# Second batch's keys in load buffers of their own, all key and value loads issued earlier, six bias groups ahead of the steps

## The chip, the cores and the metric

The kernel runs on one core of a Trainium2 chip. The metric is the device time of one launch in microseconds. The engines of the core that matter here are TensorE (PE, with its weight loads as PEld), VectorE (DVE), ScalarE (ACT), GpSimd (POOL) and SyncE (SP); nearly all transfers are issued on SP's queue, and 16 DMA engines carry them out. An engine takes its instructions strictly in the order in which they are written: this kernel is scheduled by hand, and nothing reorders it.

## The reference, cut to what matters

Three layers follow each other: attention with a learned position bias, a token and channel mixer, and a routed expert layer. The change touches the attention alone.

```python
# q, k, v: (2, 8, 576, 64): B batches, H heads, S positions, D
scores = scale * np.matmul(q, k.transpose(0, 1, 3, 2))
x = (psi_rel / psi_i)[..., None]              # of the two positions
bias = np.maximum(x @ w1 + b1, 0.0) @ w2      # (576, 576, 8 heads), 32 hidden units
scores = scores + bias.transpose(2, 0, 1)[None, :, :, :]
attn = softmax(scores)                        # row maximum, exp, row sum
out = np.matmul(attn, v)
# then the mixer (_moe_ref) and the routed experts (_moe2_ref)
```

## The kernel before, in words

**Steps.** The 576 query rows are cut into four tiles of 128 rows and a tail of 64. The tail comes first: `its` is tail, 0, 1, 2, 3. For each of the five there are eight steps, one for each pair of heads (four pairs of batch 0, then four of batch 1), so steps 0 to 7 are the tail and step 8 is the first of tile 0. A step s does the scores and softmax of its own pair, the transposes of the probabilities of step s-1, and the product with the values of step s-2 (its output transpose too). In the tail phase step s also transposes and splits the keys of pair s+2 (`key_T`, `key_split`), since those are needed for the first time then.

**Bias.** The bias of a row tile is the same for both batches. It is made in groups of 16 query rows, 36 in all: groups 0 to 3 for the tail, 4 to 11 for tile 0, and so on. `bias_hidden` makes the hidden layer of a group in four parts (`hidden0` to `hidden3`), each on DVE, ACT or POOL as `ENGINE` says. `bias_mm` multiplies it on PE (L500), ACT copies the result to an `ev` tile (L503, two `ev` buffers), and one DMA on SP (L511; two half-size ones at L509 for the tail) spreads it over the partitions of the bias tile. The softmax of a step (`softmax_tile`: DVE L337 adds the bias and takes the row extreme, ACT L340 the exponential) reads the whole bias tile of its row tile. So step 0 needs groups 0 to 3 landed, and step 8 needs groups 4 to 11.

**What sets the order.** `ORDER["start"]` is the list of work ahead of step 0, written out by hand; it holds the loads and `bias0` to `bias4`. Then each step runs a list of its phase. `AHEAD = 1` makes `ahead` = 5: five groups are done at the start and each later step does one (`gi`), so that group 11 is done in step 6 and step 7 does none. SP's queue is in order too: a DMA whose data isn't ready holds all that are written behind it. Each SP DMA also waits until the one eight places ahead of it has landed.

**Loads.** `load_k(i)` loads the keys of two pairs (five DMAs, 576 KB) into a ring of two buffers `kn`; `load_k(4)`, the first of batch 1, therefore waits for the transposes of the first keys, and `load_k(6)` for those of the second. `load_v(b)` loads the values of one batch (ten DMAs, 1152 KB). `load_q` loads queries; in step 4 the load for step 10 waits for a buffer that POOL's `tail_split` of step 5 frees. `query_rest` copies the split queries of a pair of steps into place with four DMAs (`qt<-qs`, L328).

Of the kernel before, what the change touches and what calls it, by code (L numbers as in the profile page):

```python
# [9 lines left out]
F32 = mybir.dt.float32  # L10
# [11 lines left out]
B, H, S, D = 2, 8, 576, 64  # L22
# [26 lines left out]
MROWS = E * CAP + 10 * 128  # L49

WARM = 3
AHEAD = 1
QRB = 2
TB = 2
QO = 3, 3, 3, 6

ORDER = {
    "start": "hidden0 const load_k2 tail_split0 hidden1 bias0 hidden2 bias1 key_T00 hidden3 zero key_T01 key_T11 key_T10 key_split0 tail_split1 bias2 hidden4 bias3 load_k4 hidden5 key_split1 tail_T bias4 load_v load_q".split(),
    "first": "scores0 hidden2 last_T prob_T0 values key_T0 normalize query_T tail_T query_split hidden1 hidden0 key_T1 bias_mm key_split out_T tail_split hidden3 query_rest".split(),
    "mixed": "hidden2 scores0 values tail_T query_T normalize hidden0 last_T prob_T0 key_T0 key_T1 query_split tail_split hidden1 key_split query_rest bias_mm out_T hidden3".split(),  # L60
    "bias": "query_T query_split hidden3 scores0 scores1 last_T values hidden0 query_rest hidden2 late bias_mm out_T mix prob_T0 prob_T1 hidden1 normalize".split(),
# [37 lines left out]
def body(ctx, tc, q, k, v, w1, b1, w2, wt1, wt2, wc1, wc2, wg, wl, mw1, mw2,  # L99
# [17 lines left out]
    with tc.manual_schedule():  # L117
        tok = ctx.enter_context(ExitStack())
        mix = TokenMix(nc, x)
        attention(tc, nc, tok, mix, q, k, v, w1, b1, w2, c_L, c_id, ident, x, wt1, wt2, prefill)  # L120
        if "x" in dbg:
            nc.sync.dma_start(dbg["x"], x)
        R = Routing(tc, nc, wg, wl, ident, c_tok, c_small, x2d, meta)
        X = Experts(tc, nc, R, Rings(tc, ctx, "big", side="right"), x_p, mw1, mw2, ident, x2d, meta, out)
        mixer(tc, nc, tok, mix, wc1, wc2, ident, x, R, X)
        if "x2" in dbg:
            nc.sync.dma_start(dbg["x2"], x2d)
        X.rest()
        X.close()
        R.close()  # L130


def attention(tc, nc, tok, mix, q, k, v, w1, b1, w2, c_L, c_id, ident, x, wt1, wt2, prefill):
# [9 lines left out]
    tw_p = pool(tok, "tokw")  # L143
    with ExitStack() as ctx:
        cst = pool(ctx, "acst")
        bias_p = pool(ctx, "bias", 2)
        nat_p = pool(ctx, "nat")
# [58 lines left out]


        nat = {}

        def load_k(i):  # L210

            b, pr = divmod(i, NP)
            n = nat_p.tile([128, 20, D], F32, name="kn", tag="kn", bufs=2)
            main, hs = n[:, 0:16].rearrange("p (n h) d -> p n h d", h=4), k[b, 2 * pr:2 * pr + 4]
            for j in range(NIT):
                nc.sync.dma_start(main[:, j], hs[:, 128 * j:128 * j + 128].rearrange("h p d -> p h d"))
            nc.sync.dma_start(n[0:64, 16:20], hs[:, 512:S].rearrange("h p d -> p h d"))
            for j in range(2):
                nat["k", i + j] = main[:, :, 2 * j:2 * j + 2], n[0:64, 16 + 2 * j:18 + 2 * j]

        def load_v(b):
            n = kv_p.tile([128, NIT + 1, H, D], F32, name=f"v{b}")


            nv, src = n.rearrange("p n (a e) d -> e p n a d", e=2), v[b].rearrange("(a e) p d -> e p a d", e=2)
            for e in range(2):
                r, z = (slice(64 * o, 64 * o + 64) for o in (e, 1 - e))
                nc.gpsimd.memset(nv[e][z, NIT], 0.0)
                for j in range(NIT):
                    nc.sync.dma_start(nv[e][:, j], src[e][64 * e + 128 * j:64 * e + 128 * j + 128])  # L230
                nc.sync.dma_start(nv[e][r, NIT], src[e][0:64] if e else src[e][512:S])
            nat["v", b] = n

        def load_q(it, i):

            b, pr = divmod(i, NP)
            n = nat_p.tile([128, 4, D], F32, name="qn", tag="qn", bufs=2)
            if it == NIT:
                tv = q[b, :, 512:S].rearrange("(a e) p d -> e p a d", e=2)
                for e in range(2):  # L240
                    nc.sync.dma_start(n[64 * e:64 * e + 64], tv[e])
                for j in range(NP):
                    nat["q", it, i + j] = n[:, j]
            else:
                nc.sync.dma_start(n, q[b, 2 * pr:2 * pr + 4, 128 * it:128 * it + 128].rearrange("h p d -> p h d"))
                nat["q", it, i] = n
# [271 lines left out]
        def fetch(p):  # L518
            n = p[1]
            if p[0] == 0:  # L520
                src = wt1[128 * n:min(128 * n + 128, S)]
            else:
                src = wt2[128 * n:128 * n + 128, HALF * p[2]:HALF * p[2] + HALF]
            raws[p] = fetch_f64(nc, nat_p, src, "kn", 2, p[0] == 0 and n == 4)
# [61 lines left out]
        first = NG - 8 * NIT  # L586
        ahead = first + AHEAD
        N = len(steps)
# [19 lines left out]
        def late_fetch(s):  # L608

            if pieces and any(f is decode for f, *_ in late.get(s, ())):  # L610
                fetch(pieces.pop(0))

        load_const()
        bias_setup()
        start = {
            "const": (bias_const,), "zero": (query_zero,), "load_k2": (load_k, 2), "load_k4": (load_k, 4), "load_v": (load_v, 0),
            "load_q": (load_q, *steps[NP]), "tail_T": (tail_T, *steps[0]),
        }
        for n in range(2):
# [11 lines left out]
        for s in range(N + 2):  # L631

            bias = gi < len(groups) and s < N and s >= B * NP * (its.index(groups[gi] // 8) - 1)
            at = lambda d, n=N: steps[s + d] if 0 <= s + d < n else None
            two = lambda d: (s + d) % 2 == 0 and s + d >= B * NP and at(d)
            hide = groups[gi + 1] if bias and gi + 1 < len(groups) else None
            todo = {
                "late": (late_step, (s,)), "mix": (mixes[s][0], mixes[s][1:]) if s in mixes else (None, None),
                "tail_split": (tail_split, at(2, B * NP)), "tail_T": (tail_T, at(1, B * NP)),
                "query_T": (query_T, two(QO[0])), "query_split": (query_split, two(QO[1])), "query_rest": (query_rest, two(QO[2])),  # L640
                "key_split": (key_split, at(2, B * NP)),
                "normalize": (normalize, at(0)), "last_T": (last_T, at(-1)),
                "values": (values, at(-2)), "out_T": (out_T, at(-2)),
                "bias_mm": (bias_mm, (groups[gi],) if bias else None),
            }
            for j in range(4):
                todo[f"hidden{j}"] = bias_hidden, hide is not None and (hide, (j,))
                todo[f"key_T{j}"] = key_T, j < 2 and at(2, B * NP) and (*at(2), j)
                todo[f"scores{j}"] = scores, at(0) and (*at(0), j)
                todo[f"prob_T{j}"] = prob_T, at(-1) and (*at(-1), j)  # L650
            if two(QO[3]):
                load_q(*steps[s + QO[3]])
            for name in ORDER["edge" if bias and s % (B * NP) == B * NP - 1 else "first" if s < 3 else "mixed" if s < B * NP else "bias" if bias else "plain"]:
                f, a = todo[name]
                if a:
                    f(*(a[1:] if f in (key_split, key_T) else a))
            gi += bias
            late_fetch(s - 1)
            if s == 1:
                load_k(6)  # L660
            if s == 2:
                load_v(1)
            if s == 10:
                prefill()
            if s == 8:
                for _ in range(2):
                    fetch(pieces.pop(0))
# [635 lines left out]
class Experts:  # L1303
# [6 lines left out]

    AHEAD = [[f"big{4 * a + c}.0" for c in range(4)] for a in range(2)]
    HIGH = [f"big{8 + c}.0" for c in range(4)], ["raw.0", "raw.1", "raw.2", "uT0a.0"]
    LOW = ["uT1a.0", *AHEAD[0][0:3]], [AHEAD[0][3], *AHEAD[1][0:3]]

# [11 lines left out]
    def guess(self):  # L1326
        nc = self.nc
        self.raw = [[self.place(n, F32) for n in names] for names in self.AHEAD]
        self.e = e = nc.values_load(self.R.picked[0:1, 0:1], engines=[SP], min_val=0, max_val=E - 1)
# [14 lines left out]
    def open(self):  # L1344
# [7 lines left out]
            (0, 0): cycle([*map(spot, self.HIGH[0]), own(0)]), (0, 1): cycle([*map(spot, self.LOW[0]), own(1)]),  # L1352
            (1, 0): cycle([*map(spot, self.HIGH[1]), spot(self.AHEAD[1][3])]), (1, 1): cycle([*map(spot, self.LOW[1]), own(2)]),
        }
# [408 lines left out]
```

## Time and profile before

| | |
|---|---|
| median of 3 runs | 583.69 us (582.85 to 583.7) |
| the profiled execution | 584.03 us; its span 582.3 us |
| busy share of the span: PE, DVE, ACT, POOL | 94%, 66%, 57%, 42% |
| chain that ended last, PE / DVE / DMA / issue / ACT | 65% / 12% / 7% / 5% / 5% |
| of it, bias transfers `bias<-ev` | 6% |

The busy shares are means over phases with different limits. The tail phase with its start takes the first 72 us; the four row tiles follow to about 220 us, then mixer and experts. The profile's page cuts the span into 40 slices of 14.6 us; in the first five DVE reads 5, 7, 8, 9, 5 tenths, and the page's DMA line 6, 9, 9, 7, 9. The time outside the span (584.03 less 582.3, 1.7 us) is launch and end.

### The profile page before, as it was taken

How to read it: one execution, taken by the hardware profiler on the slowest of the kernel's cores; microseconds unless marked ns; L12 is line 12 of the kernel's file. 1: busy time of each engine (PE TensorE's matmuls, PEld its weight loads, DVE VectorE, ACT ScalarE, POOL GpSimd, SP SyncE). 2: the span in 40 equal slices, each digit the busy share in tenths (PEclk: the TensorE clock that was granted, in tenths of full speed). 3: DMA queues.
4: the chain of work that ended last, by engine and by line, in shares of the span. 5: the costliest groups of instructions: out<-in, count | busy, mean ns of one | idle time of the engine just before them, and what ended most of it. 6: DMA issues, size and time to landing. Idle time of an engine off the chain costs nothing.

```text
span 582.3 us, 11959 instructions
## 1 busy us (share of the span) xinstructions
PE 545.5 (94%) x4306; PEld 430.3 (74%) x4306; DVE 383.9 (66%) x896; ACT 329.5 (57%) x608; POOL 242.1 (42%) x230
## 2 busy tenths in 40 slices
PE   7689699999899999989999999999999999999992
PEld 3366477777677887869999877787778778787871
DVE  5789588889887675698888535714473235668650
ACT  4678589789898793344444223221423257777760
POOL 4666547476555360044444300310014234657541
PEclk8979889999999999999999999999999999999997
DMA  6997988698697351143443020081002985566950
GB/s 162 130 173 126 142 158 165 132 177 157 127 147 126 77 154 38 37 138 120 148 161 126 1 91 0 1 302 61 19 18 43 370 299 175 147 230 245 367 185 12
DMA packets 72110, 79.90 MB, mean 137 GB/s; under 512 B 36822, under 2 KB 51420, under 8 KB 72044
## 3 DMA queue, kind: packets, MB, share of 16 engines
q1 hardware_dynamic: 67276, 73.72, 50.7%
q0 software_dynamic: 2176, 5.26, 2.7%
q8 instruction: 36, 0.59, 0.5%
q10 hardware_dynamic: 2592, 0.09, 0.3%
q14 instruction: 30, 0.25, 0.2%
HBM read 72.08 MB, written 5.34 MB: 133 GB/s over the span
## 4 chain that ended last, share of the span: by engine, by line
PE 65%; DVE 12%; DMA 7%; issue 5%; ACT 5%; SPq 2%; POOL 2%; ACTq 0%; POOLq 0%; DVEq 0%
PE ph L748 20%; PE po L748 16%; DMA bias<-ev 6%; PE py L748 5%; PE ps L500 5%; PE tp L425 4%; PE ps L359 3%; PE tp L410 3%; DVE t L337 2%; ACT t L340 2%; PE tp L748 1%; DVE K L272 1%; DMA mt<-meta 1%; PE tp L1448 1%; DVE raw L732 1%
## 5 line engine op out<-in xcount | busy, mean ns | idle before, releaser
L490 POOL TENSOR_SCALAR hd<-tabs,sc,negb 128x576 f32<-128x576 f32 x32 | 76.4, 2389 | 4.7 <-PE ps L500 3.0
L340 ACT ACTIVATE t<-t,st 128x576 f32<-128x576 f32 x72 | 55.4, 770 | 28.8 <-DVE st L337 28.4
L748 PE MATMUL po<-cw,h 128*128 128x512 f32 x272 | 67.3, 395 | 0.0
L337 DVE CUSTOM_DVE_ANT_0 t<-ps,bias 128x576 f32<-128x576 f32 x72 | 52.3, 751 | 16.1 <-DMA bias<-ev 6.6
L359 PE MATMUL ps<-K,qt 128*128 128x288 f32 x320 | 54.0, 309 | 4.4 <-DVE qt L199 3.5
L748 PEld LDWEIGHTS po<-cw,h 128*128 128x128 f32 x272 | 49.8, 188 | 10.0 <-issue 0.4
L1411 DVE TENSOR_TENSOR big<-raw,big 128x1024 fp32r<-128x1024 f32 x30 | 42.3, 1433 | 22.4 <-ACT big L1410 22.4
L500 PE MATMUL ps<-hd,wblk 128*32 128x288 f32 x576 | 47.7, 440 | 7.5 <-DVE st L337 6.5
L359 PEld LDWEIGHTS ps<-K,qt 128*128 128x128 f32 x320 | 45.0, 192 | 6.7 <-DVE qt L199 2.3
L425 PE MATMUL tp<-pt,v 128*64 128x128 f32 (+1 forms) x800 | 49.2, 268 | 0.6 <-DVE K L272 0.6
L748 PE MATMUL py<-big,hT 128*128 128x512 f32 x184 | 47.8, 400 | 0.4 <-POOL big L1411 0.4
L1189 POOL DMA_INDIRECT meta<-tokid,posi x10 | 10.0, 996 | 90.7 <-DVE tokid L1186 54.7
L425 PEld LDWEIGHTS tp<-pt,v 128*64 128x64 f32 x800 | 40.1, 137 | 8.1 <-issue 5.1
L1410 ACT CAST big<-raw 128x1024 fp32r<-128x1024 f32 x44 | 44.2, 1055 | 2.8 <-DMA big<-in_moe_w_dram 1.0
L748 PE MATMUL ph<-big,xT 128*128 128x512 f32 x168 | 42.9, 403 | 0.0
L490 DVE TENSOR_SCALAR hd<-tabs,sc,negb 128x576 f32<-128x576 f32 x69 | 42.2, 640 | 1.0 <-PE ps L500 0.9
L748 PEld LDWEIGHTS py<-big,hT 128*128 128x128 f32 x184 | 33.8, 188 | 8.6 <-POOL big L1411 0.9
L740 POOL TENSOR_TENSOR big<-wf,big 128x512 fp32r<-128x512 f32 x12 | 18.8, 1564 | 50.3 <-ACT big L739 50.3
L487 ACT ACTIVATE hd<-tabs,b1c,sc 128x576 f32<-128x576 f32 x43 | 36.9, 866 | 3.8 <-DVE sc L458 3.7
L1411 POOL TENSOR_TENSOR big<-raw,big 128x1024 fp32r<-128x1024 f32 x10 | 27.5, 2747 | 24.9 <-ACT big L1410 24.3
L748 PEld LDWEIGHTS ph<-big,xT 128*128 128x128 f32 x168 | 30.6, 189 | 8.6 <-issue 1.6
L500 PEld LDWEIGHTS ps<-hd,wblk 128*32 128x32 f32 x576 | 17.2, 115 | 24.1 <-DVE st L337 7.9
(302 smaller groups left out, 1204.7 us busy)
## 6 DMA issues: line engine op xcount, KB each, us to landing
raw<-in_moe_w_dram SPq DMA_DIRECT2D x48, 512.0 KB
raw<-in_moe_w_ch_dram SPq DMA_DIRECT2D x24, 512.0 KB
bias<-ev SPq DMA_DIRECT2D x32, 288.0 KB
qt<-qs SPq DMA_DIRECT2D x64, 128.0 KB
lw<-in_moe_w_dram SPq DMA_DIRECT2D x16, 512.0 KB
big<-in_moe_w_dram SPq DMA_DIRECT2D x8, 512.0 KB
lw<-in_moe_w_dram SPq DMA_DIRECT2D x16, 256.0 KB
big<-in_moe_w_dram SPq DMA_DIRECT2D x16, 256.0 KB
```

The source lines that it names most:

```text
L337: nc.vector.tensor_tensor_reduce(t.rearrange("p (a j) -> p a j", a=2), ps[:, :, 0:HALF], bs.rearrange("p (a j) -> p a j", a=2), op0=ALU.ad ...
L340: nc.scalar.activation(t, t, AF.Exp, bias=st[:, j:j + 1], scale=-1.0, accum_out=st[:, 2 + j:3 + j])
L359: nc.tensor.matmul(ps[:, hf, 0:HALF], lhsT=qt[:, j], rhs=K[k][:, hf * HALF:(hf + 1) * HALF], start=j == pairs[0][0], stop=j == pairs[-1][0])
L410: nc.tensor.transpose(tp[:, 128 * j:128 * j + 128], tt[:, o:o + 128], ident)
L425: nc.tensor.matmul(po[64 * h:64 * h + 64, 0:rhs.shape[1]], lhsT=lhsT, rhs=rhs, start=j == 0, stop=j == 4)
L487: nc.scalar.activation(hd[:, qq], Lt[:, o:o + S], AF.Relu, bias=b1c, scale=sc[:, c])
L490: eng.tensor_scalar(hd[:, qq], Lt[:, o:o + S], sc[:, c], negb, ALU.mult, ALU.max)
L500: nc.tensor.matmul(ps[32 * qq:32 * qq + 32, hf, 0:HALF], lhsT=wblk, rhs=hd[:, qq, hf * HALF:(hf + 1) * HALF], start=True, stop=True)
L740: nc.gpsimd.tensor_tensor(lo, src, hi.bitcast(F32), ALU.subtract)
L748: nc.tensor.matmul(out, lhsT=lhs[a], rhs=rhs[b], start=first and i == 0, stop=last and i == 2)
L1410: nc.scalar.copy(hi, raw)
L1411: (nc.gpsimd if c == 3 and t else nc.vector).tensor_tensor(lo, raw, hi.bitcast(F32), ALU.subtract)
```

## The change

The ring `kn` now holds only the keys of batch 0; those of batch 1 go into a new tile `later` of `tokw`, in the place (tag `w2s`) that the mixer's second token weights take from step 9 on. `load_k4` moves ahead of group 2's transfer, `load_v` ahead of group 3's, `load_k6` from the end of step 1 ahead of group 4's, and `load_v(1)` from step 2 to step 0. `AHEAD` becomes 2: group 5 and the hidden layer of group 6 are done at the start, and every tail step does the group that the next step did; step 6 does none. Group 5 counts as one of the start's for the choice of engines (`hidden_by`).

```diff
-AHEAD = 1
+AHEAD = 2
...
-    "start": "hidden0 const load_k2 tail_split0 hidden1 bias0 hidden2 bias1 key_T00 hidden3 zero key_T01 key_T11 key_T10 key_split0 tail_split1 bias2 hidden4 bias3 load_k4 hidden5 key_split1 tail_T bias4 load_v load_q".split(),
+    "start": "hidden0 const load_k2 tail_split0 hidden1 bias0 hidden2 bias1 load_k4 key_T00 hidden3 zero key_T01 key_T11 key_T10 key_split0 tail_split1 bias2 load_v hidden4 bias3 load_k6 hidden5 key_split1 tail_T bias4 load_q hidden6 bias5".split(),
...
         nat = {}
+        later = tw_p.tile([128, 2, 20, D], F32, name="kn2", tag="w2s")
...
-            n = nat_p.tile([128, 20, D], F32, name="kn", tag="kn", bufs=2)
+            n = later[:, i // 2 - 2] if b else nat_p.tile([128, 20, D], F32, name="kn", tag="kn", bufs=2)
...
-            if s == 1:
-                load_k(6)
-            if s == 2:
+            if s == 0:
                 load_v(1)
```

In the rows below `kn` are keys, `v` values, `qn` queries, `bias<-ev` a bias group's transfer. On SP's queue, around the tail's bias groups, this stood before (L509 the eight halves of groups 0 to 3, L511 group 4):

```order
L217 DMA kn<-in_k_dram 64x4x64
L509 DMA bias_185<-ev 16x4x576 x8
L216 DMA kn<-in_k_dram 128x4x64 x4
L217 DMA kn<-in_k_dram 64x4x64
L511 DMA bias_310<-ev 16x8x576
L230 DMA v_323<-in_v_dram 128x4x64 x4
L231 DMA v_323<-in_v_dram 64x4x64
```

and this stands now (all lines below the first insertion are one higher, and L510 is the tail's groups):

```order
L218 DMA kn<-in_k_dram 64x4x64
L510 DMA bias_186<-ev 16x4x576 x4
L217 DMA kn_104<-in_k_dram 128x4x64 x4
L218 DMA kn_104<-in_k_dram 64x4x64
L510 DMA bias_186<-ev 16x4x576 x2
L231 DMA v_278<-in_v_dram 128x4x64 x4
L232 DMA v_278<-in_v_dram 64x4x64
L231 DMA v_278<-in_v_dram 128x4x64 x4
L232 DMA v_278<-in_v_dram 64x4x64
L510 DMA bias_186<-ev 16x4x576 x2
```

The tail's eight transfers are cut in three: the third group stands behind the third load of keys, the fourth behind the ten loads of values too.

On SP's queue, around the last bias groups of tile 0 (steps 4 to 7; L245 loads queries, L328 puts the split queries in place), before:

```order
L245 DMA qn<-in_q_dram 128x4x64
L511 DMA bias_310<-ev 16x8x576
L328 DMA qt_104<-qs 64x2x256 x4
L511 DMA bias_310<-ev 16x8x576
L245 DMA qn<-in_q_dram 128x4x64
L511 DMA bias_310<-ev 16x8x576
L328 DMA qt_105<-qs 64x2x256 x4
```

and now:

```order
L246 DMA qn<-in_q_dram 128x4x64
L512 DMA bias_328<-ev 16x8x576
L329 DMA qt_105<-qs 64x2x256 x4
L512 DMA bias_328<-ev 16x8x576
L246 DMA qn<-in_q_dram 128x4x64
L329 DMA qt_106<-qs 64x2x256 x4
```

Behind the waiting load of queries there were three groups (9, 10, 11), and there are two (10, 11); the last now stands ahead of the next load of queries.

## Rows read from the trace of the kernel before

**Rows 1.** Busy time by stretch: PE, PEld, DVE, ACT, POOL, granted clock, DMA share, GB/s
```profile
16.00:18.00 2.00, 1.25 (x8) 0.34 (x6) 1.94 (x5) 1.14 (x2) 1.42 (x1) 1.00 0.15 25
28.00:36.00 8.00, 6.94 (x45) 4.57 (x45) 6.82 (x19) 6.17 (x11) 5.98 (x10) 0.57 1.01 170
36.00:44.00 8.00, 6.91 (x98) 5.21 (x97) 7.51 (x23) 5.69 (x12) 5.30 (x9) 1.00 1.21 169
66.00:72.00 6.00, 2.02 (x29) 1.61 (x29) 1.07 (x4) 0.98 (x2) 4.31 (x4) 0.77 1.14 140
```

**Rows 2.** Timeline of DVE around step 0: start, length, what, [idle before <- releaser]
```profile
21.19 0.29 DVE L199 TENSOR_SCALAR qt<-tp 128x128 fp32r<-128x128 f32 x1
24.44 0.76 DVE L337 CUSTOM_DVE_ANT_0 t<-ps,bias 128x576 f32<-128x576 f32 x1 [2.96 <-PE tp L262]
...
30.07 0.76 DVE L337 CUSTOM_DVE_ANT_0 t<-ps,bias 128x576 f32<-128x576 f32 x1
```

**Rows 3.** Timeline of PE: the scores of step 0
```profile
21.63 1.34 PE L359 MATMUL ps<-K,qt 128*128 128x288 f32 x8 [1.66 <-DVE qt L199]
```

**Rows 4.** Timeline of SP's queue at the start: issue, time taken by the issues
```profile
17.50 2.92 SPq L509 DMA_DIRECT2D bias<-ev  x4
...
19.23 1.18 SPq L509 DMA_DIRECT2D bias<-ev  x2
...
20.52 2.25 SPq L216 DMA_DIRECT2D kn<-in_k_dram  x4
...
24.42 2.47 SPq L230 DMA_DIRECT2D v<-in_v_dram  x4
26.93 2.46 SPq L231 DMA_DIRECT2D v<-in_v_dram  x1
29.43 2.94 SPq L230 DMA_DIRECT2D v<-in_v_dram  x4
```

**Rows 5.** Chain of waits: start, length (a DMA's from its issue)
```profile
13.46 4.91 DMA bias<-ev
...
19.83 1.33 DMA bias<-ev
...
64.14 7.37 DMA bias<-ev
```

**Rows 6.** Timeline of PE: first users of early loads
```profile
36.43 0.80 PE L425 MATMUL tp<-pt,v 128*64 128x64 f32 x20
...
49.13 0.63 PE L259 MATMUL tp<-ident,kn 128*128 128x128 f32 x4 [0.62 <-PE tp L387]
```

**Rows 7.** Timeline of DVE, steps 6 to 8
```profile
59.45 0.76 DVE L337 CUSTOM_DVE_ANT_0 t<-ps,bias 128x576 f32<-128x576 f32 x1
...
66.57 0.29 DVE L444 COPY x<-tp 64x128 f32<-64x128 f32 x1
71.73 0.76 DVE L337 CUSTOM_DVE_ANT_0 t<-ps,bias 128x576 f32<-128x576 f32 x1 [4.87 <-DMA bias<-ev]
```

**Rows 8.** Timeline of SP's queue, steps 5 to 8
```profile
57.17 0.38 SPq L245 DMA_DIRECT2D qn<-in_q_dram  x1
57.65 1.66 SPq L511 DMA_DIRECT2D bias<-ev  x1
59.48 2.66 SPq L328 DMA_DIRECT2D qt<-qs  x4
62.24 0.58 SPq L511 DMA_DIRECT2D bias<-ev  x1
62.92 0.54 SPq L245 DMA_DIRECT2D qn<-in_q_dram  x1
64.14 0.58 SPq L511 DMA_DIRECT2D bias<-ev  x1
```

**Rows 9.** Timeline of POOL, step 5: what frees the query buffer
```profile
56.82 0.32 POOL L295 TENSOR_TENSOR qm<-qn,qm 128x64 fp32r<-128x64 f32 x1
```

**Rows 10.** Timeline of PE, step 8 and the next
```profile
66.20 0.77 PE L359 MATMUL ps<-K,qt 128*128 128x288 f32 x4 [0.97 <-DMA qt<-qs]
...
72.55 2.15 PE L500 MATMUL ps<-hd,wblk 128*32 128x288 f32 x16 [4.30 <-DVE st L337]
...
78.15 1.18 PE L500 MATMUL ps<-hd,wblk 128*32 128x288 f32 x16
```

More of the change, by code (lines that the diff above doesn't have):

```diff
@@ L615, in attention @@
         start = {
-            "const": (bias_const,), "zero": (query_zero,), "load_k2": (load_k, 2), "load_k4": (load_k, 4), "load_v": (load_v, 0),
+            "const": (bias_const,), "zero": (query_zero,), "load_k2": (load_k, 2), "load_k4": (load_k, 4), "load_k6": (load_k, 6), "load_v": (load_v, 0),
             "load_q": (load_q, *steps[NP]), "tail_T": (tail_T, *steps[0]),
```

## The prediction

> **What bounds the kernel now.** I read the busy time by stretch first, to see which engine fills which part of the tail phase, then the chain of waits of that part, then the timelines of the engines that the chain names. The change moves work of the first 72 us only; from step 8 on every queue holds the same instructions in the same order, and a shift there is carried to the end whole. So the question is when the softmax of step 8 starts, 71.73 us now [rows 7].
>
> Three things set that start. First, step 0 cannot begin before the tail's bias has landed. DVE is through with its work at 21.48 and its L337 starts at 24.44; the trace names a PE transpose as the releaser [rows 2], but the scores that it reads ended at 22.97 [rows 3], and what else the instruction waits for are the transfers of the four tail groups. The last of them was issued at 19.83 [rows 5]. The chain's 1.33 us behind it ends in another instruction; I take the start of L337 as its landing, 4.6 us after the issue, which agrees with the 4.91 us of an earlier half [rows 5]. Second, from step 1 to step 6 DVE sets the pace: five steps from 30.07 to 59.45 [rows 2, 7], 5.9 us each, DVE busy 7.51 of 8 us [rows 1]. Nothing in there waits for a load: the first product with the values at 36.43 has no idle time before it, and the transpose of the last keys at 49.13 was released by PE's own work [rows 6]. Third, before step 8 DVE is idle from 66.86 to 71.73, 4.87 us, for the last bias group of tile 0 [rows 7]. That transfer is late because SP stood at the load of queries until 57.17, for POOL's split that ends at 57.14 [rows 8, 9]; behind it queue group 9 (57.65), four query copies (59.48), group 10 (62.24), a load (62.92), group 11 (64.14), which lands at 71.51, 7.37 us later [rows 5, 8]. The DMA engines are full there, 1.14 of their share at 140 GB/s [rows 1].
>
> **The change, part by part.** The early loads themselves (third and fourth load of keys, the values of batch 1) gain nothing: no user waited for them [rows 6]. The buffers of their own only let them be issued without a wait. The POOL clearing of the values' unused rows moves with them into idle time of POOL. I cost all this at zero; its cover is that the loads were early already.
>
> What is queued behind them is the price. The two halves of tail group 3 are issued from 19.23 on now, behind the pair of group 2, whose two issues fill 17.50 to 18.7 [rows 4]. In the changed queue ten loads of values stand between. Their issues take 0.56 us each if SP runs as freely as at 20.52 (2.25 us for four), 0.62 as in the first four loads of values (2.47), and 0.88 each if the queue is as full as it was (nine issues from 24.42 to 32.37) [rows 4]. Ten are 5.6, 6.2 or 8.8 us, so group 3 starts at 24.3, 24.9 or 27.5, its second half 0.6 us later, and with 4.6 us to land the softmax of step 0 starts at 29.5, 30.1 or 32.7 instead of 24.44: 5.1, 5.7 or 8.3 us late. I take 5.9, near the free end, because the DMA engines are nearly idle at 16 to 18 us (0.15) [rows 1], so the queue starts almost empty; a little is added for the keys now ahead of group 2. DVE is the engine that waits, in order, and all of the tail's steps stand behind it: **+5.9 us**, bounds +5.1 and +8.3.
>
> While it waits PE has nothing to do but group 5. In the trace the granted clock is already down to 0.57 in 28 to 36, behind PE's idle time at the start [rows 1], and a bias group on PE takes 2.15 us at the low level against 1.18 [rows 10], so a step whose PE work is long runs up to 1 us longer. A longer wait can leave the low level on for one more step, or only move it: 0 to +1.0, I take **+0.3**.
>
> Group 5 and the hidden layer of group 6 come ahead of step 0. One part is on DVE, half a microsecond in the 2.96 us (then about 8.5) that DVE is idle; the two on ACT and one on POOL lie in the same wait. Steps 0 to 5 do as much bias work as before, so the pace stays 5.9 us and the wait of step 0 reaches SP's stop in step 5 whole. Step 6 loses its group.
>
> That shift pays at step 8. Behind SP's stop there is one group less and the last one goes ahead of a load: it takes the place that group 10 has now, issued 1.9 us sooner (62.24 against 64.14) [rows 8]. The DMA engines are full, so what counts is the data taken out from ahead of it: one group and one load of queries, 288 and 128 KB, 426 thousand bytes, which at 140 GB/s are 3.0 us [rows 1]. Bounds: 1.9 by the issues, 4.87 if the whole idle time goes. What is late next is close: the query copies let PE's scores start at 66.20 [rows 10], and DVE is ready at 66.86. I take **-3.0**. A shorter stall may also spare PE the low clock that it falls into at 72.55: 2.15 us against 1.18 for the same matmuls [rows 10], 0 to -1.0; PE still idles in pieces before, so I take half, **-0.5**.
>
> The sum, against the profiled execution: 584.03 + 5.9 + 0.3 - 3.0 - 0.5 = 586.73. That execution stands 0.34 us above the median of the runs shown, so the forecast is **586.4 us**, 2.7 us slower. With all bounds to one side the sum reaches from -0.8 (5.1 + 0 - 4.87 - 1.0) to +7.4 (8.3 + 1.0 - 1.9 - 0); it is unlikely that all four fall together, and the forecast's own range is +1.2 to +5.0, 584.9 to 588.7.
>
> The Trainium skill speaks against this reading: "DMA: Bandwidth & Descriptors", section "Rules for kernel authors", says to issue a DMA early, compute meanwhile and wait late, so that its fixed cost is hidden. The trace shows what that leaves out here, that a transfer on the same queue with a nearer user is pushed back; by the rule alone the loads cost nothing and the sum would be the first rival's.
>
> **The rivals.** *Faster: the tail's last group is not held.* If the 16 engines work its packets in beside the loads of values, and SP issues those without delay, step 0 starts when DVE is ready anyway and only the gains stay: 583.7 - 3.0 - 0.5 = **580.2 us**. For it: landings overlap wherever the share is above 1 [rows 1]. Against it: the issues alone, 5.6 us and in order, put the group's issue past 24. It decides at a start of step 0 before 27.9, 3.5 us late. Chance 0.12.
>
> *No change that can be told.* Step 0 is 5.1 us late and the whole idle time of step 8 goes (4.87): 583.7 + 5.1 + 0.3 - 4.9 - 0.5, about **583.7 us**. For it: the group that now goes first behind SP's stop, 57.65, is slow to issue (1.66) in idle DMA engines [rows 8] and may be quicker. Against it: four query copies still stand ahead. Chance 0.25.
>
> *Slower still.* The queue fills as it did, 8.3 us, the clock costs its 1.0, and step 8 gains only 1.9: 583.7 + 7.4 = **591 us**. Chance 0.08.
>
> *The change does nothing:* the loads were hidden and the moved groups cancel. That would need the tail's last group unmoved on the queue, which the order rules out; it is in the case of no change.
>
> **How the numbers follow.** The forecast has 0.55. A measurement of this kernel can tell about 0.2%, 1.2 us. Faster by more: the first rival and a sliver, 0.13. Within: the second rival and the low end of the forecast, 0.27. Slower: 0.60. The range for 8 in 10 leaves out most of the first rival and of the last: 582.6 to 589.4.
>
> **What would show it.** In the changed profile: L338 of step 0 starts at 29.5 to 31, idle before it some 8 us; SP's issues of group 3 stand at 24 to 26; the L338 of step 6 comes about 6 us later than 59.45; the idle time before the L338 of step 8 is under 2 us against 4.87, and that softmax starts at about 74.5. Wrong is the argument if step 0 starts by 27, or if the steps between run faster than 5.9 us: then a load did slow them and I costed its move at nothing.

## The result, and the profile after

The changed kernel takes 586.86 us in the median against 583.26 for the kernel before on the same chips: 3.6 us more. One of its eight runs took 762.81 us at a granted clock of 0.653; it is in that median, which is 586.45 without it, and not in the ratio of 1.006, with a 95% interval of 1.004 to 1.008. Its profiled execution took 587.48 us, span 585.7. The forecast was 586.4 us, 2.7 us more.

The timeline of DVE in the changed kernel, with the columns of [rows 2] (L338 is the L337 of before; the first softmax of steps 0, 1, 2, 6 and 8):

```profile
31.55 0.76 DVE L338 CUSTOM_DVE_ANT_0 t<-ps,bias 128x576 f32<-128x576 f32 x1 [10.32 <-DMA kn<-in_k_dram]
...
37.17 0.76 DVE L338 CUSTOM_DVE_ANT_0 t<-ps,bias 128x576 f32<-128x576 f32 x1
...
44.33 0.76 DVE L338 CUSTOM_DVE_ANT_0 t<-ps,bias 128x576 f32<-128x576 f32 x1
...
67.54 0.76 DVE L338 CUSTOM_DVE_ANT_0 t<-ps,bias 128x576 f32<-128x576 f32 x1
...
75.28 0.76 DVE L338 CUSTOM_DVE_ANT_0 t<-ps,bias 128x576 f32<-128x576 f32 x1 [1.64 <-PE tp L426]
```

The trace names a load of keys as what released step 0. In a second execution (e12) it names the bias transfer, and by the trace's count of landed parts (sixteen for a transfer) the second half of group 3 is complete at 31.42. Against [rows 2, 7]: step 0 is 7.11 us late (24.44), step 6 is 8.09 late (59.45), step 8 only 3.55 late (71.73). So the tail phase lost 8.1 us and 4.5 came back before step 8. SP's queue shows where the first part stands, as in [rows 4]:

```profile
17.46 0.65 SPq L218 DMA_DIRECT2D kn<-in_k_dram  x1
18.21 1.19 SPq L510 DMA_DIRECT2D bias<-ev  x2
19.45 2.31 SPq L231 DMA_DIRECT2D v<-in_v_dram  x4
21.81 1.20 SPq L232 DMA_DIRECT2D v<-in_v_dram  x1
23.05 2.25 SPq L231 DMA_DIRECT2D v<-in_v_dram  x4
25.35 0.65 SPq L232 DMA_DIRECT2D v<-in_v_dram  x1
26.09 1.24 SPq L510 DMA_DIRECT2D bias<-ev  x2
27.37 2.31 SPq L217 DMA_DIRECT2D kn<-in_k_dram  x4
29.92 0.99 SPq L218 DMA_DIRECT2D kn<-in_k_dram  x1
31.01 0.56 SPq L512 DMA_DIRECT2D bias<-ev  x1
```

Group 3's halves are issued at 26.09, behind the ten loads of values, where they were issued at 19.23 [rows 4]; 31.55 is 4.8 us behind the second half's issue, which was 4.6 before. Group 4 follows at 31.01, behind the last keys; before, it was issued at 23.82. The timeline of ACT shows what that costs, a wait that came to 0.39 us before. These are its copies of groups 4, 5 and 6 to an `ev` buffer; each needs the buffer that the transfer two groups earlier frees:

```profile
23.80 0.74 ACT L504 ACTIVATE ev<-ps,cb 128x576 f32<-128x576 f32 x1 [2.61 <-DMA bias<-ev]
31.58 0.74 ACT L504 ACTIVATE ev<-ps,cb 128x576 f32<-128x576 f32 x1 [5.53 <-DMA bias<-ev]
38.12 0.74 ACT L504 ACTIVATE ev<-ps,cb 128x576 f32<-128x576 f32 x1 [2.95 <-DMA bias<-ev]
```

The third, group 6 in step 0, waits for group 4's transfer until 38.12, and the exponential of step 1 is behind it. So step 1 to step 2 takes 7.16 us. At the other end SP's queue reads, as in [rows 8]:

```profile
65.25 0.38 SPq L246 DMA_DIRECT2D qn<-in_q_dram  x1
65.73 0.61 SPq L512 DMA_DIRECT2D bias<-ev  x1
66.75 2.65 SPq L329 DMA_DIRECT2D qt<-qs  x4
69.50 0.58 SPq L512 DMA_DIRECT2D bias<-ev  x1
70.18 0.54 SPq L246 DMA_DIRECT2D qn<-in_q_dram  x1
```

One group less stands behind SP's stop, and step 8 starts 10.0 us after the stop ends in place of 14.6. The busy time by stretch, with the columns of [rows 1]:

```profile
16.00:18.00 2.00, 0.20 (x3) 0.00 (x1) 2.00 (x4) 0.74 (x1) 1.98 (x2) 1.00 1.18 172
...
28.00:36.00 8.00, 3.87 (x24) 2.25 (x24) 3.41 (x11) 3.52 (x6) 2.03 (x5) 0.70 1.15 164
...
66.00:72.00 6.00, 5.37 (x78) 4.30 (x77) 5.33 (x18) 3.82 (x7) 1.81 (x6) 1.00 1.00 185
```

The timeline of PE, the bias groups on either side of step 8's softmax:

```profile
76.10 1.18 PE L501 MATMUL ps<-hd,wblk 128*32 128x288 f32 x16 [0.98 <-DVE st L338]
...
80.66 1.18 PE L501 MATMUL ps<-hd,wblk 128*32 128x288 f32 x16
```

The gap that the early keys use, 16 to 18 us, is full now (1.18 against 0.15). The granted clock no longer falls at step 8, so its bias group takes 1.18 us and not 2.15 [rows 10], and the next one follows 4.56 us later in place of 5.60: by then the kernel is 2.5 us late (80.66 against 78.15). The span ends 3.4 us late.

### The profile page after: what moved, and what is told of

Read it like the earlier page. It is cut to its first block, busy times and chain, and to the rows that moved or that the text cites. A ratio compares the mean times of both kernels' runs of the same rounds, so it can differ in the third digit from the quotient of the medians.

```text
span 585.7 us, 11959 instructions
## 1 busy us (share of the span) xinstructions
PE 546.7 (93%) x4306; PEld 431.1 (74%) x4306; DVE 390.7 (67%) x895; ACT 329.7 (56%) x609; POOL 245.9 (42%) x230
## 4 chain that ended last, share of the span: by engine, by line
PE 68%; DVE 12%; DMA 6%; issue 4%; ACT 4%; SPq 2%; POOL 1%; ACTq 0%; POOLq 0%; DVEq 0%
PE ph L747 21%; PE po L747 16%; PE py L747 6%; PE tp L426 5%; DMA bias<-ev 5%; PE ps L360 4%; PE ps L501 4%; PE tp L411 3%; DVE t L338 2%; DVE K L273 1%; PE tp L747 1%; PE tp L1447 1%; DVE hd L491 1%; ACT t L341 1%; PE tp L442 1%
## 5 line engine op out<-in xcount | busy, mean ns | idle before, releaser
L338 DVE CUSTOM_DVE_ANT_0 t<-ps,bias 128x576 f32<-128x576 f32 x72 | 52.3, 751 | 20.6 <-DMA kn<-in_k_dram 10.3
L360 PE MATMUL ps<-K,qt 128*128 128x288 f32 x320 | 56.2, 317 | 2.9 <-ACT ev L504 2.4
L1410 DVE TENSOR_TENSOR big<-raw,big 128x1024 fp32r<-128x1024 f32 x30 | 47.3, 1599 | 16.1 <-ACT big L1409 16.0
L501 PE MATMUL ps<-hd,wblk 128*32 128x288 f32 x576 | 45.6, 420 | 12.1 <-ACT ev L504 5.9
L360 PEld LDWEIGHTS ps<-K,qt 128*128 128x128 f32 x320 | 46.3, 197 | 5.9 <-ACT ev L504 3.6
L504 ACT ACTIVATE ev<-ps,cb 128x576 f32<-128x576 f32 x36 | 26.5, 737 | 21.4 <-DMA bias<-ev 14.8
```

Of the source, the lines that this page charges most:

```text
L338: nc.vector.tensor_tensor_reduce(t.rearrange("p (a j) -> p a j", a=2), ps[:, :, 0:HALF], bs.rearrange("p (a j) -> p a j", a=2), op0=ALU.ad ...
L360: nc.tensor.matmul(ps[:, hf, 0:HALF], lhsT=qt[:, j], rhs=K[k][:, hf * HALF:(hf + 1) * HALF], start=j == pairs[0][0], stop=j == pairs[-1][0])
L501: nc.tensor.matmul(ps[32 * qq:32 * qq + 32, hf, 0:HALF], lhsT=wblk, rhs=hd[:, qq, hf * HALF:(hf + 1) * HALF], start=True, stop=True)
L504: nc.scalar.activation(ev.rearrange("p (a b) -> p a b", a=2), ps[:, :, 0:HALF], AF.Identity, bias=cbs[hidden_by(g).replace("P", "V")])
L1410: (nc.gpsimd if c == 3 and t else nc.vector).tensor_tensor(lo, raw, hi.bitcast(F32), ALU.subtract)
```

## The experiments

My theory was that the loss is a matter of place on SP's queue: each bias transfer behind loads arrives late, and whoever needs it, or the buffer that it frees, waits. The rivals were that the sixth group ahead is the loss, and that the loads slow the start by filling the DMA engines wherever they stand. The table has the softmax of five steps and the span from each profiled execution, in us, and the ratio of the timed runs to the kernel before on the same chip.

| kernel | step 0 | step 2 | step 3 | step 6 | step 8 | span | ratio (95%) |
|---|---|---|---|---|---|---|---|
| before | 24.44 | 36.08 | 42.16 | 59.45 | 71.73 | 582.3 | 1 |
| changed | 31.55 | 44.33 | 50.26 | 67.54 | 75.28 | 585.7 | 1.006 (1.004 to 1.008) |
| e1 sixth group alone | 24.60 | 35.90 | 46.84 | 64.44 | 72.52 | 581.1 | 1.0014 (0.9997 to 1.0032) |
| e2 loads alone | 31.66 | 42.90 | 48.84 | 66.12 | 78.00 | 590.0 | 1.014 (1.0113 to 1.0168) |
| e3 values behind group 3 | 25.67 | 42.93 | 49.04 | 66.32 | 74.19 | 584.5 | 1.0071 (1.0046 to 1.0097) |
| e4 values, keys behind group 5 | 26.70 | 37.95 | 43.96 | 65.79 | 73.92 | 583.3 | 1.0052 (1.003 to 1.0074) |
| e5 six groups, no early load | 24.07 | 36.36 | 44.66 | 61.94 | 69.65 | 581.3 | 0.9992 (0.9972 to 1.0012) |
| e6 changed, three ev buffers | 30.53 | 41.94 | 48.03 | 65.32 | 73.03 | 582.9 | 1.0046 (1.0026 to 1.0066) |
| e7 changed, group 3 on ACT | 26.19 | 43.25 | 49.19 | 66.47 | 74.62 | 586.0 | 1.0076 (1.0048 to 1.0104) |
| e8 changed, last keys earlier | 34.04 | 45.28 | 51.22 | 68.52 | 76.14 | 588.4 | 1.0093 (1.0067 to 1.0118) |
| e9 values in two halves | 26.68 | 37.94 | 47.59 | 64.88 | 72.89 | 581.8 | 0.9959 (0.9944 to 0.9975) |
| e10 e9 with three ev buffers | 27.60 | 39.48 | 45.57 | 62.85 | 70.52 | 583.2 | 0.9963 (0.9939 to 0.9987) |

**The two halves of the change apart.** e1 is the kernel before with `AHEAD = 2` and `hidden6 bias5` at the end of the start list; e2 the changed kernel without them.

```diff
-AHEAD = 1
+AHEAD = 2
-... tail_T bias4 load_v load_q"
+... tail_T bias4 load_v load_q hidden6 bias5"
```

> The kernel before with the sixth bias group ahead of the steps and nothing else (no load moves, keys of batch 1 in the old ring). My theory, that the loss comes from the tail groups' transfers being queued behind the loads, and that the sixth group pays at step 8: step 0's softmax starts at 24.3 to 25, the idle time before step 8's softmax falls from 4.87 to under 2 us; group 5's transfer is now behind the ten loads of values, so ACT may wait up to 3 us for its buffer in step 1. Net 580 to 582.5 us. Rival, that the sixth group itself is the loss (more work ahead of step 0): 586 us or more, with step 0 on time. Rival, that the stall at step 8 goes elsewhere: 583 to 584 us.

> The changed kernel with five groups ahead as before, so the loads alone are moved. My theory: step 0's softmax starts at 31 to 32 (7 us late), and the stall before step 8 is still 4 to 5 us since SP's stop in step 5 moves along; 589 to 591 us. Rival, that early loads are free and the sixth group is the loss: 583 to 584 us.

e2 decides it: the loads alone cost 1.4%, with step 0 at 31.66 and the stall of step 8 still whole, one line of DVE's timeline:

```profile
78.00 0.76 DVE L338 CUSTOM_DVE_ANT_0 t<-ps,bias 128x576 f32<-128x576 f32 x1 [4.83 <-DMA bias<-ev]
```

From step 6 to step 8 the kernels with five groups take 12.28 (before) and 11.88 us (e2), those with six between 7.62 and 8.15 in the other ten rows of the table: the sixth group is worth 4 us at that place and the loads have no part in it. But e1 did not come out at 580 to 582.5 us (583.87). Its group 5 stands behind the ten loads of values, and ACT's timeline shows the same new wait as above, larger than the 3 us that I allowed:

```profile
39.31 0.74 ACT L503 ACTIVATE ev<-ps,cb 128x576 f32<-128x576 f32 x1 [5.09 <-DMA bias<-ev]
```

So the 4.2 us won before step 8 are lost ahead of it: step 2 to step 3 takes 10.94 us in place of 6.08, step 8 comes 0.8 us later than before, and the sixth group alone makes no difference that can be told.

**Loads moved behind the groups.** e3 puts the values right behind group 3, e4 puts them and the last keys behind group 5.

```diff
-... bias2 load_v hidden4 bias3 load_k6 hidden5 ... bias4 load_q hidden6 bias5"
+... bias2 hidden4 bias3 load_v load_k6 hidden5 ... bias4 load_q hidden6 bias5"   (e3)
+... bias2 hidden4 bias3 hidden5 ... bias4 load_q hidden6 bias5 load_v load_k6"   (e4)
```

> The changed kernel with the ten loads of values moved from ahead of the tail's group 3 to right behind it; they and the last keys stay ahead of group 4. My theory: step 0's softmax starts at 24.5 to 26, but group 4's transfer lands only at 34 to 36, ACT waits 5 us or more for that buffer in step 0, and step 2's softmax is still 3 to 6 us later than the 36.08 of before: the hold moves from step 0 to step 1, 582 to 586 us. Rival, that only the order ahead of group 3 counts: step 0 and all steps on time, 579 to 581 us. Rival, that the loads slow the start by filling the DMA engines wherever they stand: step 0 at 29 or later, 586 us or more.

> The changed kernel with the values of batch 0 and the last keys moved behind all six groups (the third load of keys stays ahead of group 2). My theory: step 0's softmax at 24.5 to 26, no ACT wait over 2 us for a group's transfer in steps 0 and 1, values landed just in time for step 2, the stall before step 8 under 2 us: 578.5 to 581 us, faster than both kernels. Rival, that the values now come too late for step 2: PE waits there 2 us or more, 582 us or more.

In e3 step 0 comes at 25.67, though the loads stand right behind group 3: 5.9 of the 7.1 us are the values in front of it, and the loads do not hold step 0 wherever they stand. The 1.2 us that are left are another wait, for PE's scores and not for group 3, which is complete at 24.81. With six groups ahead, group 5's product stands before the scores, and they need the buffer in PSUM (one of two) that ACT empties with its copy of group 4. That copy waits for group 2's transfer, which is behind the keys. ACT, PE and DVE of e3:

```profile
23.50 0.74 ACT L504 ACTIVATE ev<-ps,cb 128x576 f32<-128x576 f32 x1 [2.68 <-DMA bias<-ev]
24.30 1.33 PE L360 MATMUL ps<-K,qt 128*128 128x288 f32 x8 [2.54 <-ACT ev L504]
25.67 0.76 DVE L338 CUSTOM_DVE_ANT_0 t<-ps,bias 128x576 f32<-128x576 f32 x1 [4.54 <-PE ps L360]
```

The hold then moves to group 4's `ev` buffer, and in e4 on to group 7's, whose transfer is behind the last keys and the values of batch 1; step 4 to step 5 takes 9.37 us there, a place that my expectation left out. ACT's timeline of e3:

```profile
36.73 0.74 ACT L504 ACTIVATE ev<-ps,cb 128x576 f32<-128x576 f32 x1 [7.43 <-DMA bias<-ev]
```

And ACT's timeline of e4:

```profile
53.52 0.74 ACT L504 ACTIVATE ev<-ps,cb 128x576 f32<-128x576 f32 x1 [4.83 <-DMA bias<-ev]
```

e3 took 587.21 us, above the 586 expected, and its step 2 is 6.9 us late where 3 to 6 were expected. e4 was to beat both kernels and did not.

**What the hold is made of.** e6 gives the changed kernel a third `ev` buffer, e7 issues group 3's halves on ACT's queue, e8 puts the last keys ahead of group 3 as well.

```diff
-ev = nat_p.tile([128, S], F32, name="ev", bufs=2)
+ev = nat_p.tile([128, S], F32, name="ev", bufs=3)                             (e6)
-nc.sync.dma_start(bv[:, 0], ev[e::2])
+(nc.scalar if g == groups[3] else nc.sync).dma_start(bv[:, 0], ev[e::2])      (e7)
-... load_v hidden4 bias3 load_k6 hidden5 ..."
+... load_v load_k6 hidden4 bias3 hidden5 ..."                                 (e8)
```

> The changed kernel with three ev buffers in place of two, so that ACT's copy of group 6 in step 0 need not wait for group 4's transfer. My theory: step 0 still at 31.5 (the hold there is the queue's order), but step 1 to step 2 takes 5.6 to 6.1 us in place of 7.16; 1 us less than the changed kernel. Rival, that the longer step comes from TensorE's low clock there: step 1 to step 2 still 7 us, no change.

> The changed kernel with the two halves of the tail's group 3 issued on ACT's queue in place of SP's. If the hold is SP's order alone (the loads' issues and what stands in its queue): the issue stands at 19.5 to 20.5 and step 0's softmax starts at 24.5 to 26.5. If the hold is the DMA engines, busy with the loads whoever issues: step 0 at 29 or later. In the first case group 4 is still behind the loads, so ACT waits in step 0 for its buffer and step 2 comes at 42 to 44, and the time falls by 0 to 2 us only against the changed kernel.

> The changed kernel with the five loads of the last keys moved ahead of the tail's group 3 as well: the suspected cost made larger by 576 KB. My theory: step 0's softmax 2.7 to 3.5 us later than in the changed kernel (34.2 to 35), ACT's wait for group 4 shorter, step 2 about 1.5 to 2.5 us later, the time 1.5 to 2.5 us above the changed kernel. Rival, that step 0 waits for the DMA engines' total work in the start and not for its place in the queue: step 0 unchanged within 0.5 us.

e6: step 1 to step 2 takes 5.79 us in place of 7.16, and the ratio falls by 0.0014, 0.8 us, which the intervals do not keep apart. Step 0 came 1.0 us earlier too, at 30.53 where 31.5 was expected, since group 3 is issued at 25.27 there; no run tells whether the third buffer did that. The low clock is no rival for the longer step: between these two softmaxes the granted clock is 0.94 in the changed kernel (first line) and only 0.61 in e6 (second line; columns as in [rows 1]):

```profile
37.17:44.33 7.16, 5.69 (x49) 3.64 (x45) 4.89 (x15) 5.99 (x10) 4.69 (x7) 0.94 0.77 109
36.15:41.94 5.79, 5.79 (x39) 3.58 (x39) 4.88 (x14) 4.60 (x8) 4.50 (x7) 0.61 1.20 153
```

e7: the halves are issued at 19.34 on ACT, and step 0 starts at 26.19. So 5.4 us of the 7.1 go with the place on SP's queue. What is left is again PE's scores, as in e3, and not shown to be the DMA engines. The second half of group 3 did land later after its issue, 5.8 us against 4.4 before by the trace's count of landed parts, but it was complete at 25.86, ahead of step 0. Nor are the loads quite the same: SP's first four issues of values take 6.06 us in place of 2.31. The time did not fall, since group 4 is behind the loads still (ACT waits 7.23 us for it). The timelines of SP's and ACT's queue, and of DVE:

```profile
17.86 1.53 SPq L510 DMA_DIRECT2D bias<-ev  x2
...
19.34 1.34 ACTq L510 DMA_DIRECT2D bias<-ev  x2
...
19.45 6.06 SPq L231 DMA_DIRECT2D v<-in_v_dram  x4
...
26.19 0.76 DVE L338 CUSTOM_DVE_ANT_0 t<-ps,bias 128x576 f32<-128x576 f32 x1 [5.29 <-PE ps L360]
```

The Trainium skill, "DMA: Bandwidth & Descriptors", section "Issuing engines are not separate DMA queues", says that issuing from several engines saves only the sequencer's time to issue. Here that time, with what stands in the queue, was 5.4 us for one transfer, more than the 4.8 us that its second half took to land in the changed kernel.

e8: 576 KB more ahead of group 3 cost step 0 another 2.5 us (34.04), a little under the expected 2.7. Group 4 then stands right behind group 3 and step 1 to step 2 is 5.62 us, so step 2 is only 0.95 us later than in the changed kernel (1.5 to 2.5 expected); the ratio is 0.0033 above it, 1.9 us, in the range, though the intervals overlap.

**Versions that might beat both.** e5 is e1 with `load_v` behind `bias5`. e9 splits the values: their first half goes into the queue's gap behind group 1, the second with the third load of keys behind group 5; e10 adds the third `ev` buffer. (`load_va` and `load_vb` are five of the ten loads each.)

```diff
-... bias1 key_T00 ... bias3 load_k4 hidden5 ... bias4 load_v load_q hidden6 bias5"   (e1)
+... bias1 key_T00 ... bias3 load_k4 hidden5 ... bias4 load_q hidden6 bias5 load_v"   (e5)
+... bias1 load_va key_T00 ... bias3 hidden5 ... bias4 load_q hidden6 bias5 load_vb load_k4"   (e9)
```

> The sixth group ahead without any early load: the kernel before with AHEAD = 2, group 5 at the end of the start list, and the values of batch 0 moved behind it; keys stay in the old ring. My theory, that each loss of the earlier runs is a bias transfer (or the ev buffer that it frees) queued behind loads: step 0 at 24.4 to 25, step 2 at 36 to 36.5, no ACT wait over 2 us for a group's transfer in steps 0 to 4, step 8's softmax at 67.5 to 69.5; 578.5 to 581 us, faster than the kernel before. Rival, that the values now land too late for step 2: PE waits there 2 us or more, 582 us or more.

> Six groups ahead, the loads placed by what the earlier runs showed: the first half of batch 0's values goes into the gap of SP's queue behind the tail's group 1, the second half and the third load of keys behind group 5, the rest as in the kernel before. My theory: the half in the gap costs step 0 about 1 to 2 us (25.5 to 26.5), as the third load of keys did there; PE no longer waits for values in step 2, which takes 5.6 to 6.2 us; step 8's softmax at 67.5 to 70; 580 to 582.5 us, 1 to 3 us faster than the kernel before. Rival, that the start is bound by the bytes to be loaded by step 2 however they are ordered: step 2 still late by 2 us or more (38 or later), step 8 at 69.7 or later, no gain over the run with the values behind group 5.

> The same with three ev buffers, so that ACT waits for no group's transfer in the tail steps. If ev waits still hold steps there: 0.5 to 2 us less than with two. If not: no difference.

> The run with the values in two halves again, for a second profile: its first profiled execution took 583.54 us, the slowest of its twelve (median 581.29). If the wait for keys in step 2 differs between executions: an execution near 581 us has step 3's softmax at 44 to 45 in place of 47.59. If the difference lies behind the attention: step 3 again at 47 to 48 and step 8 again near 73, with a shorter rest.

e5 wins 2.1 us by step 8 and the timed runs show no difference. The rival came true in part: PE waits for the values in step 2, in three pieces of 0.26 to 0.39 us by its timeline, with DVE idle 2.17 us for it, and step 2 to step 3 takes 8.3 us. In e9 the values are in time and the keys are late:

```profile
37.97 0.80 PE L425 MATMUL tp<-pt,v 128*64 128x64 f32 x20
38.70 0.44 PE L259 MATMUL tp<-ident,kn 128*128 128x128 f32 x2
40.09 0.47 PE L259 MATMUL tp<-ident,kn 128*128 128x128 f32 x1 [0.95 <-DMA kn<-in_k_dram]
42.31 0.48 PE L259 MATMUL tp<-ident,kn 128*128 128x128 f32 x1 [1.75 <-DMA kn<-in_k_dram]
```

PE is at its low clock behind these waits (the next bias group takes 2.15 us, and 1.18 in e11), and step 2 to step 3 takes 9.65 us where 5.6 to 6.2 were expected. Still e9 is faster than both kernels: 581.29 us against 583.60 for the kernel before, ratio 0.9959. Its profiled execution was the slowest of its twelve (583.54). In a second one (e11), at 582.85 us, the keys cost 1.25 us, step 3 starts at 44.16 and step 8 at 69.50, 2.2 us before the kernel before:

```profile
40.14 0.33 PE L259 MATMUL tp<-ident,kn 128*128 128x128 f32 x1 [0.88 <-DMA kn<-in_k_dram]
...
41.06 0.25 PE L262 MATMUL tp<-ident,kn 64*128 64x64 f32 x1 [0.37 <-DMA kn<-in_k_dram]
...
69.50 0.76 DVE L337 CUSTOM_DVE_ANT_0 t<-ps,bias 128x576 f32<-128x576 f32 x1 [1.98 <-DMA bias<-ev]
```

The wait for keys differs between executions of one program. A third buffer (e10) adds nothing.

> The changed kernel again, for a second profile. My theory of the hold: step 0 at 31 to 32, step 1 to step 2 over 7 us, step 8 at 74.5 to 76 again; the rest from step 8 to the end may differ by 1 to 2 us between executions.

The changed kernel again, in a second execution (586.92 us): step 0 at 31.42, step 1 to step 2 6.79 us, a little under the 7 expected, step 8 at 75.05, span 585.1. The hold is the same within 0.4 us.

## Why the prediction was right, point by point

**The early loads at zero.** Right as far as their users go, and that term hid nothing: e2 has the loads alone, and its steps from step 1 on run at the pace of before (28.84 us from step 1 to step 6, 29.38 before; most of the difference is step 1 to step 2, 5.62 against 6.01).

**The hold of step 0, +5.9.** Right in mechanism, short in size: 7.11, inside the bounds of 5.1 to 8.3. The largest mis-sized piece is the keys ahead of group 2, for which I added "a little": SP's issues of them end at 18.11, and group 2 is issued at 18.21 and not 17.50. Then ten issues of values take 6.55 us (0.65 each) where I had 0.62, and the landing 4.8 us where I had 4.6. So three of the signs foretold were passed: step 0 at 31.55 (29.5 to 31), group 3's issue at 26.09 (24 to 26) and step 6 late by 8.1 (about 6).

**The low clock, +0.3.** The wrong cause for a real loss. Step 1 to step 2 lengthened by 1.15 us, but for ACT's wait on the `ev` buffer behind group 4's transfer; e6 removes it at a lower clock. The prediction followed who reads the landed bias and did not follow who needs the buffer that a transfer frees, two groups later. The same wait, unforeseen, ate the gain of e1 and e4.

**The pace of 5.9 us.** From step 2 to step 6 23.21 us against 23.37: as forecast.

**The gain at step 8, -3.0.** Larger: 4.54 from step 6 to step 8. The order of things was right (the last group takes the place of the one before it), the size was not: I counted only the data taken out ahead of the last group and used the issues as a bound, but both came. Counted from the end of SP's stop, the last group is issued after 4.25 us in place of 6.97 [rows 8], and step 8 starts 5.8 us behind that issue in place of 7.6. Of the 2.7 us in the issues, 0.8 are the first group behind SP's stop, issued in 0.61 us in place of 1.66 [rows 8], the reason that the second rival gave. That part is not shown to be the change's: e2, with five groups, takes 0.89. The idle time before step 8 is 1.64 us, under 2 as foretold.

**The clock at step 8, -0.5.** I took half of 1.0 and all of it came: 1.18 against 2.15.

The terms that were short cancel: +7.11 and +0.98 up to step 6, -4.54 and -1.04 after it make +2.5, where the sum was +2.7. That the sum came so close is partly luck: the losses were 1.9 us too small and the gains 2.1. Between there and the end the lateness grows, to 3.4 us in the one profiled execution and from 2.3 to 2.8 in the other. The forecast took it as carried whole, and the traces show that only within some 4 us: from the softmax of step 8 to the end of the span the fourteen traces take 508.6 (e1) to 512.7 us (e10), and two executions of the program of e9 take 508.9 and 511.6. What makes this difference was not tried.

**The rivals.** The faster one falls: step 0 did not start before 27.9. The second came true in its gain (4.5 of 4.9) and not in its hold (5.1), the third in neither. Taken as the rule of the Trainium skill that it stood for ("DMA: Bandwidth & Descriptors", "Rules for kernel authors", issue early and wait late), e2 measures what the rule leaves out, 1.4%.

## What to carry to other kernels

Before a load is issued earlier, list what stands behind it on its queue, and for each such transfer two waits: the reader of what lands, and the writer of the buffer that the transfer empties. Where the DMA engines are nearly full (shares of 1.0 to 1.2 here), an early load only chooses who waits; the place to fill is a gap in the queue, and the two kernels with a load split to fit it (half the values, e9 and e10) are the only ones here that beat the kernel before. And where one stretch gives back as the other takes, test the halves of a change apart: here the loads alone cost 1.4%, some 8 us, and the sixth group beside them gave more than 4 of it back, though alone it was worth nothing that can be measured.

## What was not expected of the hardware

The same program's loads land differently from one execution to the next: in e9 PE waited 2.7 us for a load of keys in one and 1.25 us in the other (e11), with the queue's order the same. And a first transfer behind a pause of SP was slow to issue, 1.66 us before and 0.61 us after, with the DMA engines idle both times (0.19 of their share from 56 to 60 us before, 0.01 from 60 to 66 after). In the twelve other traces it takes 0.58 to 0.89 us, so the 1.66 stands alone; no run tells why.
